# RetNet attention and a gated MLP on one core: the two heads of a pair change places in every second chunk

## The chip, the cores and the metric

The kernel runs on one core of a Trainium2 chip. The core has TensorE (PE; its weight loads are listed as PEld), VectorE (DVE), ScalarE (ACT), GpSimd (POOL) and a sync engine (SP) that issues most DMAs. The metric is the device time of one execution in microseconds; lower is better.

## The reference

Eight sequences of 576 positions with 8 heads of 64 go through a retention layer: scores with a decay per head, no softmax. The result, 512 wide, goes through a gated MLP whose gate mixes the positions of a sequence, with a residual.

```python
gamma = 1.0 - 2.0 ** (-5.0 - np.arange(H))
Dmat = np.where(rel >= 0, gamma[:, None, None] ** rel, 0.0)
x = concat_heads(np.matmul(scale * np.matmul(q, k.T) * Dmat, v))   # 8 x 576 x 512
h = gelu_tanh(x @ w_in)                                            # 512 -> 1024
u, v = h[..., :512], h[..., 512:]
v_n = (v - mean(v)) / sqrt(var(v) + 1e-6) * g_ln
v_s = einsum('ts,bsd->btd', w_sg, v_n) + b_sg[None, :, None]       # over positions
out = x + (u * v_s) @ w_out
```

## The kernel before, in words

**Blocks and chunks.** The positions are walked in 18 blocks of 256 rows. Blocks 0 and 9 are lead blocks: they hold the first 64 positions of four sequences each (32 partitions a sequence). Every other block holds 256 positions of one sequence, two blocks a sequence. A block's rows lie on 128 partitions, two neighbouring positions (a = 0, 1) on each. Partitions 0 to 63 are the block's chunk c = 0, partitions 64 to 127 its chunk c = 1, 128 positions each.

**Loads** (lines 76 to 91). Tile qk holds q and k of a block in float32, vf holds v. For a normal block each of q, k and v is one DMA of 512 KB into all 128 partitions, issued by SP (line 91); a lead block takes four DMAs of 128 KB, 32 partitions each (line 87; for block 0 the last two of q and of k go by ACT's queue). The pool has three buffers, and block j + 4 is loaded while block j is worked on: q first, k and v later in the step.

**Casts** (lines 257 to 274). GpSimd multiplies q and k by tables of decay powers, gq and gk, one value for each position and head, and writes bf16; v is copied to bf16. From block 3 on all of it is GpSimd's, in the order of the program, among small power operations for the norm (line 405, tile rs).

**Transposes.** q and k are needed with the head dimension on partitions. Two heads h = 2 kk + r, the pair kk, fill the 128 partitions: r = 0 on 0 to 63, r = 1 on 64 to 127. PE does it for the early blocks and for most of k (line 282, T); for q from block 5 and for k of the last three blocks it is a transposing DMA on SP (line 297, turn), which waits for the cast.

**Retention.** Four groups of products on PE use tiles of 64 by 64 of the 128 by 128 array. The row half of a tile is the half of the partitions that the operands are on, the column half is the half of the output's partitions.
- Sc (line 332): scores inside a chunk, rows r, columns c, so all four tiles. DVE multiplies them by the mask into ret (line 336).
- Z (line 357): adds k-transposed times v to a running state z in PSUM, a 64 by 64 matrix a head; head r on partitions 64 r to 64 r + 63. After each chunk the state is copied to bf16, tile zb (line 255, copy), by ACT for blocks below 5 and above 12 and by DVE between.
- inter (line 373): state times query, zb with qT into the output ot, chunk by chunk. Rows r and columns r for both chunks: two of the four tiles.
- intra (line 384): ret times v, added to ot; rows c, columns r.

ACT then copies ot to xT (line 390), the input of the MLP, with head r on its half of the partitions.

**MLP.** V (line 398) projects to the gate, U (line 460) to u, W (line 480) mixes positions, O (line 501) projects out and adds x (line 505, or on DVE at line 509).

**Order.** The order is written out by hand, and each engine works in that order. Lines 539 to 665 start the pipeline; the loop at lines 671 to 716 does for each block j: the transposing DMA of q of block j + 2, loads of block j + 4, intra(j), Sc and Z of the first chunk of j + 1, the cast of q of j + 3, then V, W and O pieces (run), U, inter(j + 1), Sc and Z of the second part, the casts of k and v. SP takes loads, transposing DMAs and stores in one queue.

Of the kernel before, what the change touches and what calls it, by code (L numbers as in the profile page):

```python
# [11 lines left out]
F32 = mybir.dt.float32  # L12
# [7 lines left out]
def kernel(  # L20
# [12 lines left out]
    nc = tc.nc  # L33
    B, H, S, D = q.shape
# [7 lines left out]
    NB = B // GB * NPG  # L42
# [5 lines left out]
    consts = ctx.enter_context(tc.tile_pool(name="consts", bufs=1))  # L48
# [13 lines left out]
    def place(j):  # L62

        gr, w = divmod(j, NPG)
        return (gr, None, 0) if w == 0 else (gr, GB * gr + (w - 1) // 2, (w - 1) % 2)

    def chunk(j, c):

        gr, b, half = place(j)
        if b is None:  # L70
            return 2 * gr + c, MID
        return b // 2, (MID + 1) * (b % 2) + 2 * half + c

    loaded = {}

    def load(j, parts=(k, q, v)):
        if j not in loaded:
            loaded[j] = ld.tile([128, 2, H, 2, D], F32, name="qk"), ld.tile([128, H, 2, D], F32, name="vf")
        qk, vf = loaded[j]
        gr, b, half = place(j)  # L80
        for dst, src in ((qk[:, 1], k), (qk[:, 0], q), (vf, v)):
            if src not in parts:
                continue
            if b is None:
                for x in range(GB):
                    eng = nc.scalar if j == 0 and x >= 2 and src is not v else nc.sync
                    eng.dma_start(dst[32 * x:32 * x + 32], src[GB * gr + x, :, :LEAD, :].rearrange(
                        "h (p a) d -> p h (a d)", a=2))
            else:
                s0 = LEAD + 256 * half  # L90
                nc.sync.dma_start(dst[:], src[b, :, s0:s0 + 256, :].rearrange("h (p a) d -> p h (a d)", a=2))  # L91

    load(0, (k, q))

# [32 lines left out]
    gq = consts.tile([128, 3, 2, H], F32, name="gq")  # L127
    gk = consts.tile([128, 3, 2, H], F32, name="gk")
    nc.scalar.activation(gk[:], prod[:], Act.Exp, scale=-1.0)
    nc.scalar.activation(gq[:], prod[:], Act.Exp, bias=lsc[:])  # L130
    load(0, (v,))
    w_stage = {}
    for half in (1, 0):
# [26 lines left out]
    wT = [consts.tile([128, S + LEAD], BF, name=f"wT{j}") for j in range(SB - 1)]  # L160
    wL = [consts.tile([128, S], BF, name=f"wL{e}") for e in range(2)]
    bp = consts.tile([SB * 2, 3, 64], BF, name="bp")

    def clear_wL():
        nc.gpsimd.memset(wL[0][64:], 0.0)
        nc.gpsimd.memset(wL[1][:64], 0.0)
        nc.gpsimd.memset(wnat[:, :, 0:64], 0.0)
# [31 lines left out]
    def build_wT(j):  # L199
        c0 = {"L0": 64, "L1": 0}.get(j) if isinstance(j, str) else 64 + LEAD + 128 * j  # L200
        tp = psS.tile([128, S], BF, name="wtp", tag="att")
        for t in range(SB):
            n = min(128, S - 128 * t)
            nc.tensor.transpose(tp[:, 128 * t:128 * t + n], wnat[:n, t, c0:c0 + 128], ident[:n, :n])
        if j == "L0":
            nc.vector.tensor_copy(wL[0][:64, :S - LEAD], tp[:64, LEAD:])
            nc.vector.tensor_copy(wL[0][:64, S - LEAD:], tp[:64, :LEAD])
        elif j == "L1":
            nc.vector.tensor_copy(wL[1][64:], tp[64:])
        else:  # L210
            e = nc.vector if j else nc.scalar
            copy(e, wT[j][:, :S], tp[:])
            copy(e, wT[j][:, S:], tp[:, :LEAD])
# [27 lines left out]
    xTs, uTs, gTs, vns, zbs = {}, {}, {}, {}, {}  # L241

    def xT(p, m):

        b = 2 * p + (m > MID)
        if m == MID:
            if (p, m) not in xTs:
                xTs[p, m] = xup.tile([128, KK, 128], BF, name="xm")
            return xTs[p, m]
        if b not in xTs:  # L250
            xTs[b] = xup.tile([128, MID, KK, 128], BF, name="xT")
        return xTs[b][:, m % (MID + 1)]

    def copy(eng, o, i):
        (eng.copy if eng is nc.scalar else eng.tensor_copy)(o, i)  # L255

    def cast(j, part, eng):
        s = blk.setdefault(j, {})
        qk, vf = loaded[j]
        b, half = place(j)[1:]  # L260
        kind = 0 if b is None else 1 + half
        if part == "q":
            dst, src, tab = w2.tile([128, 2, H, D], BF, name="qb"), qk[:, 0], gq
        else:
            pool = consts if b is None else w3
            dst = pool.tile([128, 2, H, D], BF, name=part + ("lead" if b is None else "b"))
            src, tab = (qk[:, 1], gk) if part == "k" else (vf[:], None)
        s[part + "b"] = dst
        o = dst[:].rearrange("p a h d -> p h a d")
        if tab is None:  # L270
            copy(eng, o, src)
        else:
            eng.tensor_tensor(o, src, tab[:, kind].rearrange("p a h -> p h a").unsqueeze(3).to_broadcast(  # L273
                [128, H, 2, D]), op=Alu.mult)
# [66 lines left out]
    def Z(j, c):  # L341

        gr, b, half = place(j)
        if b is None or (half, c) == (1, 1):
            nb = GB * gr if b is None else b + 1
            if c == 0 or nb == GB * (gr + 1):
                return
            src, lo, n, first = blk[NPG * gr], 32 * (nb % GB), 32, True
            zcur[0] = psZ.tile([128, KK, D], F32, name="zp")
        else:  # L350
            src, lo, n, first = blk[j], 64 * c, 64, False
        z, rows = zcur[0], slice(lo, lo + n)
        for a in range(2):
            for kk in range(KK):
                for r in range(2):
                    h = 2 * kk + r
                    nc.tensor.matmul(z[64 * r:64 * r + 64, kk, :], src["kb"][rows, a, h, :], src["vb"][rows, a, h, :],  # L357
                                     start=(first and a == 0 and kk == 0), stop=True, skip_group_check=True)
        zb = w3.tile([128, KK, D], BF, name="zb")
        copy(nc.scalar if j < 5 or j > NB - 6 else nc.vector, zb[:], z[:])  # L360
        zbs[(j, 1) if c == 0 else (j + 1, 0)] = zb

    def inter(j):
        s = blk[j]
        qT = s["qT"]
        s["ot"] = ot = [psO.tile([128, KK, 2, 64], F32, name="ot") for _ in range(2)]
        if place(j)[1] is None:
            return
        for kk in range(KK):
            for c in range(2):  # L370
                for r in range(2):
                    rr = slice(64 * r, 64 * r + 64)
                    nc.tensor.matmul(ot[c][rr, kk], zbs[j, c][rr, kk, :], qT[rr, :, kk, 64 * c:64 * c + 64],  # L373
                                     start=(kk == 0), stop=False, skip_group_check=True)

    def intra(j):
        s = blk[j]
        ret, vb, ot = s["ret"], s["vb"], s["ot"]
        ks = [(kk, a) for kk in (2, 3, 0, 1) for a in range(2)]
        for kk, a in ks:  # L380
            for c in range(2):
                for r in range(2):
                    cc = slice(64 * c, 64 * c + 64)
                    nc.tensor.matmul(ot[c][64 * r:64 * r + 64, kk], vb[cc, a, 2 * kk + r, :],  # L384
                                     ret[cc, r, kk, a, :],
                                     start=(place(j)[1] is None and (kk, a) == ks[0]),
                                     stop=True, skip_group_check=True)
        for c in range(2):
            x = xT(*chunk(j, c)).rearrange("p k (t a) -> p k a t", a=2)
            copy(nc.vector if j < 3 and c == 1 else nc.scalar, x, ot[c][:])  # L390
# [128 lines left out]
    def run(n):  # L519
        for _ in range(n):  # L520
            if wo:
                wo.pop(0)()

    def release(j):
        b, half = place(j)[1:]
        if b is None or half == 0:
            return
        ws = [lambda b=b, c=c, h=h: W(b, c, h) for h in range(2) for c in range(KK)]
        os = wo[2:]
        del wo[2:]  # L530
        while ws or os:
            wo.extend(ws[:2] + os[:1])
            ws, os = ws[2:], os[1:]
        p, e = divmod(b, 2)
        for m in ([MID] if e else []) + [(MID + 1) * e + x for x in range(MID)]:
            wo.append(lambda p=p, m=m: O(p, m))
# [18 lines left out]
    cast(1, "k", nc.gpsimd)  # L555
    spin(9)
    inter(0)
    intra(0)
    load(3)
    cast(1, "q", nc.vector)  # L560
# [19 lines left out]
    T(2, "k")  # L580
    spin(3)
    intra(1)
    T(2, "q")
    cen_of[0]()
# [50 lines left out]
    cast(3, "v", nc.gpsimd)  # L635
    build_wT(wb[4])
    build_wT(wb[5])
    release(2)
    run(1)
    T(3, "k")  # L640
# [112 lines left out]
```

## Time and profile before

| | |
|---|---|
| median of 3 runs | 222.45 us (220.46 to 222.47) |
| profiled execution: its time | 220.28 us |
| profiled execution: its span | 218.5 us |
| PE, DVE, POOL, ACT busy | 94%, 73%, 61%, 59% of the span |
| granted TensorE clock | 1.0 throughout |
| DMA moved | 47.47 MB, mean 217 GB/s |
| q and k loads of normal blocks | 16 each, 512 KB, median 6.2 and 7.0 us from issue to landing |

A row of a timeline or of a list of groups reads: start, duration, engine, line, operation, output<-inputs, shape, count. In a list of groups the parts behind the bars are busy time and mean ns of one, then the idle time of the engine before and what ended it. A row of the table of windows gives the stretch in us, its length, busy time of PE, PEld, DVE, ACT and POOL with counts, the granted clock, the DMA share and GB/s. The DMA share is the mean number of packets in flight over 16 engines, so it can be over 1.

### The profile page before, as it was taken

The numbers are of one execution on the slowest core, as the hardware profiler recorded it, in microseconds if no ns is written. First come the engines' busy times: TensorE is split into PE (matmuls) and PEld (weight loads), VectorE is DVE, ScalarE is ACT, GpSimd is POOL, SyncE is SP. The second block draws the span as 40 slices with busy tenths as digits, with TensorE's granted clock in tenths as the row PEclk, the third lists the DMA queues.
The fourth block names the chain that finished last, engine by engine and source line by source line (L and its number), as shares of the span: only waits on it lengthen the run. The fifth ranks groups of instructions, "written<-read, shape, count | busy, mean of one in ns | idle before, by whom it ended". The sixth has DMA issues, their size and how long they took to land.

```text
span 218.5 us, 8020 instructions
## 1 busy us (share of the span) xinstructions
PE 204.6 (94%) x3396; PEld 145.9 (67%) x3433; DVE 160.6 (73%) x347; ACT 128.3 (59%) x212; POOL 132.3 (61%) x136
## 2 busy tenths in 40 slices
PE   7897889898999999999999999999999999999990
PEld 2355567676777786777677776777867776676650
DVE  5467868785799798379857885858765887887771
ACT  5344468726577674947494948676667565465100
POOL 5187967899899598719582876758483911123000
PEclk9999999999999999999999999999999999999999
DMA  6999999999999899889979999989999982802335
GB/s 169 270 312 282 328 253 254 282 285 259 191 260 290 202 211 223 267 143 315 221 216 222 218 206 217 319 171 312 208 201 261 178 167 48 243 3 48 144 91 201
DMA packets 88180, 47.47 MB, mean 217 GB/s; under 512 B 26000, under 2 KB 82640, under 8 KB 88144
## 3 DMA queue, kind: packets, MB, share of 16 engines
q1 hardware_dynamic: 85440, 45.10, 90.2%
q0 software_dynamic: 1472, 1.20, 3.4%
q10 hardware_dynamic: 1232, 0.66, 1.2%
q8 instruction: 27, 0.44, 0.9%
q14 instruction: 9, 0.07, 0.1%
HBM read 32.79 MB, written 9.44 MB: 193 GB/s over the span
## 4 chain that ended last, share of the span: by engine, by line
PE 73%; DMA 6%; POOL 5%; issue 4%; DVE 4%; SPq 2%; ACT 2%; ACTq 1%; DVEq 0%; POOLq 0%
PE wp L480 17%; PE op L501 14%; PE hu L460 13%; PE hv L398 11%; DMA qk<-in_k_dram 4%; PE ot L384 4%; PE sc L332 4%; PE zp L357 4%; PE ot L373 3%; DMA qk<-in_q_dram 2%; PE op L505 2%; PE tp L282 2%; SPq L91 2%; POOL wnat L197 1%; POOL rs L405 1%
## 5 line engine op out<-in xcount | busy, mean ns | idle before, releaser
L405 POOL TENSOR_TENSOR rs<-rs,mhalf 128x1 f32<-128x1 f32 x36 | 31.6, 879 | 60.4 <-DVE rs L413 60.3
L336 DVE TENSOR_TENSOR ret<-sc,mask 128x512 bf16<-128x512 f32 x72 | 46.1, 682 | 11.9 <-PE sc L332 11.5
L480 PE MATMUL wp<-wT,vn 128*128 128x288 bf16 x256 | 41.7, 287 | 0.1
L482 DVE TENSOR_TENSOR gT<-wp,uT 128x288 bf16<-128x288 f32 x64 | 27.9, 450 | 12.8 <-PE wp L480 12.1
L460 PEld LDWEIGHTS <-w_in 128*128 128x128 bf16 x576 | 34.1, 98 | 3.2 <-issue 0.5
L501 PE MATMUL op<-w_out,gT 128*128 128x512 bf16 (+1 forms) x133 | 34.6, 373 | 1.1 <-issue 0.5
L409 DVE BATCH_NORM_STATS2 bst<-vg 128x6 f32<-128x512 f32 x36 | 24.8, 689 | 13.3 <-ACT vg L401 13.2
L460 PE MATMUL hu<-xT,w_in 128*128 128x128 bf16 x512 | 33.7, 219 | 0.2 <-DVE gT L482 0.2
L398 PE MATMUL hv<-w_in,xT 128*128 128x512 bf16 x111 | 31.5, 379 | 1.3 <-ACT xT L255 0.5
L273 POOL TENSOR_TENSOR kb<-qk,gk 128x1024 bf16<-128x1024 f32 x16 | 31.4, 1963 | 1.3 <-DMA qk<-in_k_dram 1.3
L401 ACT ACTIVATE vg<-hv 128x512 f32<-128x512 f32 x36 | 21.4, 595 | 15.4 <-PE hv L398 15.3
L422 DVE SCALAR_TENSOR_TENSOR vc<-vg,mv,g_bc 128x512 f32<-128x512 f32 x36 | 29.6, 823 | 0.0
L480 PEld LDWEIGHTS <-vn 128*128 128x128 bf16 x256 | 23.8, 98 | 8.0 <-ACT vn L434 0.7
L273 POOL TENSOR_TENSOR qb<-qk,gq 128x1024 bf16<-128x1024 f32 x15 | 28.9, 1928 | 0.0
L434 ACT ACTIVATE vn<-vc,rs 128x512 bf16<-128x512 f32 x32 | 23.1, 725 | 8.3 <-POOL rs L405 7.8
L463 ACT ACTIVATE uT<-hu 128x512 bf16<-128x512 f32 x32 | 19.2, 600 | 9.1 <-PE hu L460 8.9
L255 ACT CAST xT<-ot 128x512 bf16<-128x512 f32 x30 | 20.1, 740 | 6.4 <-PE ot L384 6.2
L501 PEld LDWEIGHTS <-gT 128*128 128x128 bf16 x148 | 12.9, 98 | 11.1 <-issue 0.3
L507 ACT COPY ob<-op 128x512 f32<-128x512 f32 x23 | 13.5, 588 | 10.6 <-PE op L505 10.4
L398 PEld LDWEIGHTS <-xT 128*128 128x128 bf16 x128 | 11.9, 98 | 9.9 <-DVE xT L255 0.5
L332 PE MATMUL sc<-qT,kT 64*64 64x128 bf16 x576 | 17.2, 219 | 1.4 <-DVE qT L255 0.7
L480 PE MATMUL wp<-wL,vnm 128*128 128x288 bf16 x64 | 18.4, 287 | 0.0
(104 smaller groups left out, 279.4 us busy)
## 6 DMA issues: line engine op xcount, KB each, us to landing
qk<-in_k_dram SPq DMA_DIRECT2D x16, 512.0 KB, 7.0
qk<-in_q_dram SPq DMA_DIRECT2D x16, 512.0 KB, 6.2
vf<-in_v_dram SPq DMA_DIRECT2D x16, 512.0 KB, 7.6
out_dram<-ob SPq DMA_DIRECT2D x20, 256.0 KB, 4.7
out_dram<-obs SPq DMA_DIRECT2D x11, 256.0 KB, 2.6
wst<-in_moe_w_in_dram SPq DMA_DIRECT2D x2, 1024.0 KB, 7.5
vf<-in_v_dram SPq DMA_DIRECT2D x8, 128.0 KB, 4.6
out_dram<-ob SPq DMA_DIRECT2D x8, 128.0 KB, 3.2
```

Of the source, the lines that this page charges most:

```text
L273: eng.tensor_tensor(o, src, tab[:, kind].rearrange("p a h -> p h a").unsqueeze(3).to_broadcast([128, H, 2, D]), op=Alu.mult)
L332: nc.tensor.matmul(sc[r][cc, x, a, :], kT[rr, a, kk, cc], qT[rr, :, kk, cc], start=True, stop=True, skip_group_check=True)
L336: nc.vector.tensor_tensor(s["ret"][:, r, 2 * g:2 * g + 2], sc[r][:], msk[:].unsqueeze(1).to_broadcast([128, 2, 2, 128]), op=Alu.mult)
L398: nc.tensor.matmul(hv[:], xT(p, m)[:, kk], w_in[:, kk, F2:], start=(kk == 0), stop=(kk == KK - 1))
L405: nc.gpsimd.tensor_tensor(st["rs"][:], st["rs"][:], mhalf[:], op=Alu.pow)
L409: nc.vector.bn_stats(bst[:], vg[:])
L422: nc.vector.scalar_tensor_tensor(vc[:], vg[:], mv[:, 0:1], g_bc[:], op0=Alu.subtract, op1=Alu.mult)
L434: nc.scalar.mul(vn[:], vc[:], rs[:])
L460: nc.tensor.matmul(hu[:, c, :], w_in[:, kk, 128 * c:128 * c + 128], xT(p, m)[:, kk], start=(kk == 0), stop=(kk == KK - 1), skip_group_chec ...
L480: nc.tensor.matmul(ps[:], vns[p, m][e][:, 128 * c:128 * c + 128], w, start=(x == 0), stop=(x == SB - 1))
L482: nc.vector.tensor_tensor(gTs[p][:, c, col:col + HS], ps[:], uTs[b][:, c, half * HS:half * HS + HS], op=Alu.mult)
L501: nc.tensor.matmul(op[:], gTs[p][:, c, r], w_out[:, c, f], start=(c == 0), stop=(xn is not None and c == KK - 1), skip_group_check=True)
```

## The change

For the normal blocks from block 4 on (TURNED), the two heads of each pair change places in the second chunk of q and k: on partitions 64 to 127 head 2 kk + 1 stands where 2 kk stood. The DMA does it: each q or k load becomes one DMA for partitions 0 to 63 and two for partitions 64 to 127, one for the even and one for the odd places. v stays. The tables of decay powers get a copy with the same exchange (turn_tables, six copies on GpSimd after the cast of v of block 3). Z takes k from the other place. The state that meets the second chunk is copied with its halves exchanged, in two copies of 64 partitions: one on the engine that copied it before, one on ACT. In inter the second chunk then has rows r and columns 1 - r, so its products use the other two tiles of the array. intra reads ret from the other place, and ot, xT and all behind it are as before.

```diff
+    TURNED = 4
+    def turned(j, c):
+        return c if j >= TURNED and place(j)[1] is not None else 0
...
-                nc.sync.dma_start(dst[:], src[b, :, s0:s0 + 256, :].rearrange("h (p a) d -> p h (a d)", a=2))
+                rows = src[b, :, s0:s0 + 256, :].rearrange("h (p a) d -> p h (a d)", a=2)
+                if j < TURNED or src is v:
+                    nc.sync.dma_start(dst[:], rows)
+                    continue
+                nc.sync.dma_start(dst[:64], rows[:64])
+                for r in range(2):
+                    nc.sync.dma_start(dst[64:, r::2], rows[64:, 1 - r::2])
...
+    def turn_tables():
+        for n, src in enumerate((gq, gk)):
+            gx[id(src)] = dst = consts.tile([128, 2, 2, H], F32, name=f"gx{n}")
+            nc.gpsimd.tensor_copy(dst[:64], src[:64, 1:])
+            for r in range(2):
+                nc.gpsimd.tensor_copy(dst[64:, :, :, r::2], src[64:, 1:, :, 1 - r::2])
...
+        if tab is not None and turned(j, 1):
+            tab, kind = gx[id(tab)], half
...
-                    nc.tensor.matmul(z[64 * r:64 * r + 64, kk, :], src["kb"][rows, a, h, :], src["vb"][rows, a, h, :],
+                    nc.tensor.matmul(z[64 * r:64 * r + 64, kk, :],
+                                     src["kb"][rows, a, h if first else 2 * kk + (r ^ turned(j, c)), :],
+                                     src["vb"][rows, a, h, :],
...
-        copy(nc.scalar if j < 5 or j > NB - 6 else nc.vector, zb[:], z[:])
+        eng = nc.scalar if j < 5 or j > NB - 6 else nc.vector
+        if c == 0 and turned(j, 1):
+            copy(eng, zb[:64], z[64:])
+            copy(nc.scalar, zb[64:], z[:64])
+        else:
+            copy(eng, zb[:], z[:])
...
-                    nc.tensor.matmul(ot[c][rr, kk], zbs[j, c][rr, kk, :], qT[rr, :, kk, 64 * c:64 * c + 64],
+                    e = 64 * (r ^ turned(j, c))
+                    nc.tensor.matmul(ot[c][e:e + 64, kk], zbs[j, c][rr, kk, :], qT[rr, :, kk, 64 * c:64 * c + 64],
...
-                                     ret[cc, r, kk, a, :],
+                                     ret[cc, r ^ turned(j, c), kk, a, :],
...
     build_wT(wb[5])
+    turn_tables()
```

More of the change, by code (lines that the diff above doesn't have):

```diff
@@ L130 @@
     nc.scalar.activation(gq[:], prod[:], Act.Exp, bias=lsc[:])
+    gx = {}
     load(0, (v,))
```

## The prediction, made before the changed kernel ran

> **What bounds the kernel now.** I read the page first (busy shares, slices, chain), then the PE timeline around one state-query product, then the table of windows for the DMA, then SP's timeline with the landings.
>
> ```profile
> span 218.5 us, 8020 instructions
> ...
> PE 204.6 (94%) x3396; PEld 145.9 (67%) x3433; DVE 160.6 (73%) x347; ACT 128.3 (59%) x212; POOL 132.3 (61%) x136
> ...
> PE   7897889898999999999999999999999999999990
> ...
> DMA  6999999999999899889979999989999982802335
> ...
> PE 73%; DMA 6%; POOL 5%; issue 4%; DVE 4%; SPq 2%; ACT 2%; ACTq 1%; DVEq 0%; POOLq 0%
> ```
>
> TensorE is busy in nine tenths or more of every slice from 55 us to 205 us and carries 73% of the chain, so a saving on PE there is a saving in time as long as nothing else is late. The second thing to see is the DMA row: eight or nine tenths in nearly every slice until about 175 us, although DMA has only 6% of the chain. It is nearly a second bound, hidden by loads that are issued a step early.
>
> The profiled execution took 220.28 us, 1.8 more than its span; it lies 2.2 below the median of 222.45 and close to the lowest run, 220.46. My sum starts from 220.28. A difference under about 1% (2.2 us) can't be told from no change here.
>
> **The saving.** One call of inter, with the scores and state products behind it, and a product elsewhere that fills all four 64x64 tiles of the array:
>
> ```profile
> 85.02 0.52 PE L373 MATMUL ot<-qT,zb 64*64 64x128 bf16 x12
> 85.33 0.24 PE L332 MATMUL sc<-qT,kT 64*64 64x128 bf16 x2
> ...
> 85.43 0.22 PE L373 MATMUL ot<-qT,zb 64*64 64x128 bf16 x2
> ...
> 86.06 1.04 PE L501 MATMUL op<-w_out,gT 128*128 128x512 bf16 x3
> ```
> ```profile
> 92.09 0.39 PE L332 MATMUL sc<-qT,kT 64*64 64x128 bf16 x16
> ```
>
> Today both chunks use the two diagonal tiles of the array, so 16 products start as 8 pairs: 85.02 to 85.43 in 7 steps, 0.058 us a pair. The four-at-once pattern that inter gets is the one that L332 has already: 16 products in 0.39, less 0.22 for the last one's own duration, 3 steps of 0.057. So a call shrinks from 8 steps to 4, by 0.23 us. What must be subtracted is overlap: the first L332 products start at 85.33, on the idle tiles, before inter ends. But the diagonal tiles still have their own L332 and L357 work afterwards, so L501 at 86.06 waits for them; shortening the diagonal's queue by 4 steps moves L501 by all of it. Blocks 4 to 17 without the lead block 9 are 13 calls: 13 x 0.23 = 3.0 us.
>
> [...]
>
> **Edits on other engines.**
>
> ```profile
> L255 ACT CAST zb<-zp 128x256 bf16<-128x256 f32 x18 | 6.8, 377 | 11.1 <-PE zp L357 11.1
> L454 POOL COPY uT<-um 128x256 bf16<-128x256 bf16 x8 | 3.1, 393 | 0.0
> L172 POOL CAST bp<-left 10x64 bf16<-10x64 f32 x2 | 0.5, 226 | 0.1
> ```
> ```profile
> 46.93 1.93 POOL L273 TENSOR_TENSOR qb<-qk,gq 128x1024 bf16<-128x1024 f32 x1
> ```
> ```profile
> 49.62 0.61 PE L282 MATMUL tp<-ident,qb 128*128 128x128 bf16 x8
> ```
>
> The 13 split copies of zb keep 256 elements per partition, so each half lasts as long as a whole: 13 x 0.377 = 4.9 us more on ACT; DVE, where it had a whole copy, has a half of the same length. ACT is 59% busy and mostly waits for PE; the state is read only after a projection and a gate product. I take 0; without that cover it is up to +4.9. The halves stand behind the xT copies, so ACT does not wait for Z where it didn't before; what queues behind is the next gate or ob, 0.4 later. The changed indices in Z, intra and the casts cost nothing: same shapes, same counts.
>
> The six table copies stand on POOL ahead of block 4's casts. From 226 ns at 64 elements and 393 at 256 I get about 198 at 32 and 184 at 16: 2 x 198 + 4 x 184 = 1.13 us (ends: 0 and 6 x 393 = 2.4). POOL finishes qb(4) at 48.86 and PE transposes it at 49.62: cover 0.76, so +0.37 us (ends 0 and 1.6).
>
> **The loads, which decide.** Each q and k load from block 4 on becomes three DMAs: partitions 0 to 63, then twice partitions 64 to 127 with half the heads. That is 52 more issues on SP. The rows that resemble them are the lead loads, 128 KB into 32 partitions:
>
> ```profile
> 77.50 1.93 SPq L87 DMA_DIRECT2D vf<-in_v_dram  x4
> ```
> ```profile
> 2.50:3.50 1.00, 1.00 (x4) 0.39 (x3) 0.93 (x4) 0.80 (x1) 1.00 (x3) 1.00 1.13 329
> 77.00:82.00 5.00, 5.00 (x110) 4.27 (x109) 4.86 (x11) 3.59 (x6) 4.79 (x7) 1.00 1.11 203
> 106.00:111.00 5.00, 4.95 (x78) 3.50 (x77) 4.02 (x10) 3.22 (x6) 3.74 (x3) 1.00 1.21 291
> 30.00:50.00 20.00, 18.72 (x324) 14.86 (x324) 16.39 (x39) 12.71 (x23) 16.02 (x17) 1.00 1.11 275
> 50.00:70.00 20.00, 19.11 (x407) 14.28 (x410) 16.17 (x34) 13.54 (x24) 18.77 (x15) 1.00 1.15 245
> 70.00:90.00 20.00, 19.75 (x347) 14.73 (x340) 16.21 (x35) 13.74 (x23) 15.35 (x16) 1.00 1.09 232
> 90.00:110.00 20.00, 19.79 (x332) 14.61 (x335) 15.02 (x32) 12.65 (x22) 12.56 (x10) 1.00 1.03 228
> 110.00:130.00 20.00, 19.57 (x369) 14.69 (x371) 15.30 (x35) 13.75 (x23) 13.01 (x12) 1.00 1.01 208
> 130.00:150.00 20.00, 19.58 (x372) 14.59 (x374) 13.71 (x30) 15.10 (x26) 12.76 (x12) 1.00 1.08 249
> 150.00:170.00 20.00, 19.84 (x374) 15.00 (x375) 13.46 (x31) 13.04 (x24) 12.21 (x10) 1.00 1.15 230
> ```
>
> The last two columns are the DMA share and GB/s. From 106 to 111 us only whole 128-partition loads run: 291 GB/s at a share of 1.21, the engines full. From 77 to 82 us the lead's k and v parts run one after another from SP: 203 GB/s, though the engines are hardly less occupied (1.11) and the issue (0.48 us for 128 KB, some 270 GB/s) is faster. From 2.5 to 3.5 us the same kind of parts come from two queues at once, SP filling the first 64 partitions and ACT the last 64: 329 GB/s. So neither size nor source makes them slow; a stream into one half of the partitions is slow. A split load fills one half, then the other: 524 KB at 203 is 2.58 us against 1.80 at 291, +0.78 (ends: 0, and no row gives more). 26 loads: +20.3 us of DMA time.
>
> [...]
>
> What can hide it: the seven windows from 30 to 170 us have a mean share of 1.09; against 1.21 that leaves 140 x (1 - 1.09/1.21) = 14 us spare. Spare can be used only where a load is already issued, so 14 is its upper end. By 166 us, 13.6 of it has passed and the queue is 20.3 - 13.6 = 6.7 us late. Who waits next:
>
> ```profile
> 166.38 3.54 SPq L297 DMA_TRANSPOSE kT<-kb  x1
> ...
> 174.77 1.29 SPq L297 DMA_TRANSPOSE kT<-kb  x1
> ```
> ```profile
> kT<-kb SPq DMA_TRANSPOSE x1, 5.5
> ```
> ```profile
> 174.24 0.39 PE L332 MATMUL sc<-qT,kT 64*64 64x128 bf16 x16
> ```
>
> kT of block 16 is issued behind the loads, lands at 166.38 + 5.5 = 171.9 and is read at 174.24: slack 2.4. So the scores of block 16 come 6.7 - 2.4 = 4.3 us late. Whatever inter has saved before that point is spent waiting; only the calls of blocks 16 and 17 come after it, 2 x 0.23 = 0.5. Sum: 4.3 - 0.5 = +3.8, 224.1 us. The table copies and part of the waiting fall earlier and are inside that number. The early sign of it is qT of block 5:
>
> ```profile
> 52.62 1.34 SPq L297 DMA_TRANSPOSE qT<-qb  x1
> ```
> ```profile
> DMA to landing us min/median/max: 6.3/6.3/6.3
> ```
> ```profile
> 60.27 0.39 PE L332 MATMUL sc<-qT,kT 64*64 64x128 bf16 x16
> ```
>
> Seven split loads stand ahead of it, 7 x 0.78 = 5.5 us, less 1.7 spare before 50 us (20 x (1 - 1.11/1.21)): 3.8 late against a slack of 60.27 - 58.9 = 1.4, so about 2.4 us of PE waiting there.
>
> **The rivals.** (1) Loads keep the whole-load rate; the saving arrives: -3.0 + 0.4 = -2.6, 217.7 us. For it: DMA has only 6% of the chain, so loads are rarely waited for. Against it: the 203 GB/s row. It needs an extra under about 0.2 us a load. (2) The slowness of the lead parts is a price per DMA, (0.65 - 0.45) = 0.2 us for each extra one (128 KB at 203 against 291): 52 x 0.2 = 10.4 in all. With half of the spare used, 6.8, the end is 3.6 - 2.4 = 1.2 late, less 0.5: +0.7, 221.0 us; with all of it used, (1)'s time. Against it: the engines stay occupied between the parts, share 1.11. (3) ACT becomes the late one: 13 x 0.377 = 4.9 in full, less 2.6: +2.3, 222.6. It decides from the point where the gate's PSUM tiles come free late; ACT's 41% idle speaks against it. (4) Four at once does not come about: inter's 0.23 stays, the DMA's lateness remains, 224.6.
>
> **How the numbers follow.** Forecast and (4), which end in the DMA, 0.5 and 0.03; (1) 0.2; (2) 0.2; (3) 0.07. The range takes (1) at its lower end, 217.6. At the upper end half of the spare can't be used: 4.3 + 6.8 - 0.5 = +10.6, 231. The forecast's own range is 221.5 to 231. Faster by over 1% is (1): 0.2. Within 1%: (2) and a little of the forecast's low end, 0.25. Slower: 0.55.
>
> **What would show it.** In the changed profile: L373 in a span of about 0.4 with four starts per 0.057 (saving right); ACT zb at 377 ns in halves; windows of q and k loads near 200 GB/s, and q and k landings later by a growing amount; waits of POOL casts for DMA of several us; PE waiting at L332 near 60 and 175 us. If split loads run at 290 GB/s, the forecast is wrong and (1) holds.

## The result and the profile after

The changed kernel took 237.09 us in the median of all its runs (233.31 to 239.16, 4 runs), the kernel before 221.57 beside it. The ratios here and below leave out executions in a disturbed, slower state, which here are two of the four runs, the profiled one (238.78 us) among them, so amounts below are taken from the experiments where they can be. The ratio of the other two (233.31 and 235.40) is 1.058 with an interval of 1.044 to 1.072. The forecast was 224.1, with 231 as its upper end.

The page of the changed kernel:

```profile
span 236.9 us, 8115 instructions
...
PE 207.3 (87%) x3396; PEld 145.4 (61%) x3433; DVE 161.2 (68%) x347; ACT 133.7 (56%) x225; POOL 132.4 (56%) x142
...
PE   8697798989459999999999979989999469999992
...
PEclk9999999999758999999999999999999959999999
DMA  6999999999999999999999999999999992452227
...
PE 40%; DMA 16%; DVE 14%; POOL 9%; ACT 9%; issue 5%; SPq 4%; ACTq 1%; DVEq 0%; POOLq 0%
```

PE's busy time is 2.7 us more than before while the span grew by 18.4: PE does hardly more work, it waits, and in two places, near 60 us and near 190 us (the 45 and the 46 in its row). In both the granted clock falls as well, to 0.50 from 63 to 72 us and from 189 to 195. The DMA row is full from the second slice to the thirty-third; before, it had eights and sevens in it.

PE's timeline, at these two places and at one ordinary call of inter:

```profile
67.52 0.64 PE L355 MATMUL sc<-qT,kT 64*64 64x128 bf16 x16 [3.46 <-ACT xT L276]
...
95.40 0.42 PE L404 MATMUL ot<-qT,zb 64*64 64x128 bf16 x16
95.65 0.39 PE L355 MATMUL sc<-qT,kT 64*64 64x128 bf16 x16
...
191.75 0.64 PE L355 MATMUL sc<-qT,kT 64*64 64x128 bf16 x16 [5.23 <-DMA kT<-kb]
```

Block 5's scores come at 67.52 (before 60.27), block 16's at 191.75 (before 174.24). Between them the call of inter does what the change says: 0.42 from the first start to the last end, less 0.22 for the last product's own duration, is 0.20 for 16 products, where before they took 0.42 from first start to last.

The list of waits (total, times, longest, us), and the table of windows:

```profile
DVE ret L359 <- PE sc L355: 23.8, 13, 7.6
...
ACT vn L465 <- POOL rs L436: 14.0, 10, 6.1
...
POOL qb L296 <- DMA qk<-in_q_dram: 7.1, 2, 5.4
ACT zb L276 <- DVE zb L276: 6.8, 6, 2.0
...
PE sc L355 <- DMA kT<-kb: 5.2, 1, 5.2
...
PE sc L355 <- ACT xT L276: 3.5, 1, 3.5
...
PE op L532 <- DMA w_out<-in_moe_w_out_dram: 2.9, 1, 2.9
```
```profile
43.00:53.00 10.00, 9.08 (x208) 7.14 (x206) 7.20 (x14) 4.13 (x7) 9.77 (x13) 1.00 1.20 191
50.00:70.00 20.00, 12.61 (x251) 9.35 (x255) 9.36 (x19) 8.45 (x15) 14.62 (x13) 0.82 1.24 186
67.00:69.50 2.50, 1.64 (x34) 1.39 (x36) 1.29 (x2) 1.01 (x2) 2.50 (x3) 0.50 1.21 191
```

The list names ACT's copy xT as what ended PE's wait of 3.5 us for block 5's scores. POOL and ACT around 60 us:

```profile
55.91 1.03 POOL L276 CAST vb<-vf 128x1024 bf16<-128x1024 f32 x1
62.29 1.93 POOL L296 TENSOR_TENSOR qb<-qk,gx 128x1024 bf16<-128x1024 f32 x1 [5.35 <-DMA qk<-in_q_dram]
...
64.52 0.56 POOL L436 TENSOR_TENSOR rs<-rs,mhalf 128x1 f32<-128x1 f32 x1
```
```profile
65.11 0.72 ACT L465 ACTIVATE vn<-vc,rs 128x512 bf16<-128x512 f32 x1 [6.12 <-POOL rs L436]
...
66.68 1.33 ACT L276 CAST xT<-ot 128x512 bf16<-128x512 f32 x2
```

POOL stands at q of block 6, which has not landed and which PE doesn't use until much later. Behind it in POOL's queue is a small power operation (rs) of another block; ACT's vn waits for that; and behind vn in ACT's queue is the copy xT. So one late load holds up two queues. But PE's scores don't need xT: in the kernel before they start at 60.27, while the products (L384, 59.80 to 60.44) that xT copies are still running. What they need is qT of block 5. Its transposing DMA is issued at 61.42 here (52.62 before) and takes 6.0 us to land, at 67.4, when the first of the two xT copies ends as well. So the wait is the one for qT, as in the run with the loads alone below, and the copies hide behind it: they are done at 68.0, and their reader, V, starts at 70.62. The wait for w_out just ahead (2.9) hides in it too: without it PE would have stood longer at the scores.

### The profile page after: what moved, and what is told of

It reads as the page before. It is cut to its first block, busy times and chain, and to the rows that moved or that the text cites. A ratio compares the mean times of both kernels' runs of the same rounds, so it can differ in the third digit from the quotient of the medians.

```text
span 236.9 us, 8115 instructions
## 1 busy us (share of the span) xinstructions
PE 207.3 (87%) x3396; PEld 145.4 (61%) x3433; DVE 161.2 (68%) x347; ACT 133.7 (56%) x225; POOL 132.4 (56%) x142
## 4 chain that ended last, share of the span: by engine, by line
PE 40%; DMA 16%; DVE 14%; POOL 9%; ACT 9%; issue 5%; SPq 4%; ACTq 1%; DVEq 0%; POOLq 0%
PE op L532 10%; PE wp L511 9%; PE hu L491 6%; DMA qk<-in_q_dram 6%; PE hv L429 6%; DMA qk<-in_k_dram 4%; DVE ret L359 4%; POOL kb L296 3%; DVE bst L440 3%; DMA kT<-kb 3%; DVE vc L453 3%; POOL rs L436 2%; SPq L100 2%; DVE gT L513 2%; DMA vf<-in_v_dram 2%
## 5 line engine op out<-in xcount | busy, mean ns | idle before, releaser
L436 POOL TENSOR_TENSOR rs<-rs,mhalf 128x1 f32<-128x1 f32 x36 | 30.9, 859 | 71.1 <-DVE rs L444 71.1
L511 PE MATMUL wp<-wT,vn 128*128 128x288 bf16 x256 | 42.8, 291 | 0.9 <-ACT ob L538 0.6
L532 PE MATMUL op<-w_out,gT 128*128 128x512 bf16 (+1 forms) x133 | 35.3, 379 | 4.7 <-DMA w_out<-in_moe_w_out_dram 2.9
L429 PE MATMUL hv<-w_in,xT 128*128 128x512 bf16 x111 | 32.6, 391 | 1.4 <-ACT xT L276 0.5
L296 POOL TENSOR_TENSOR qb<-qk,gx 128x1024 bf16<-128x1024 f32 x13 | 25.1, 1931 | 7.1 <-DMA qk<-in_q_dram 7.1
L453 DVE SCALAR_TENSOR_TENSOR vc<-vg,mv,g_bc 128x512 f32<-128x512 f32 x36 | 29.0, 808 | 0.0
L296 POOL TENSOR_TENSOR kb<-qk,gx 128x1024 bf16<-128x1024 f32 x13 | 25.1, 1931 | 0.1
L276 ACT CAST xT<-ot 128x512 bf16<-128x512 f32 x30 | 20.1, 737 | 7.3 <-PE ot L415 7.2
L355 PE MATMUL sc<-qT,kT 64*64 64x128 bf16 x576 | 15.4, 223 | 9.7 <-DMA kT<-kb 5.2
L276 ACT CAST zb<-zp 64x256 bf16<-64x256 f32 (+1 forms) x31 | 11.4, 368 | 22.0 <-PE zp L380 15.0
```

The costliest lines, as they stand in the source:

```text
L429: nc.tensor.matmul(hv[:], xT(p, m)[:, kk], w_in[:, kk, F2:], start=(kk == 0), stop=(kk == KK - 1))
L436: nc.gpsimd.tensor_tensor(st["rs"][:], st["rs"][:], mhalf[:], op=Alu.pow)
L453: nc.vector.scalar_tensor_tensor(vc[:], vg[:], mv[:, 0:1], g_bc[:], op0=Alu.subtract, op1=Alu.mult)
L511: nc.tensor.matmul(ps[:], vns[p, m][e][:, 128 * c:128 * c + 128], w, start=(x == 0), stop=(x == SB - 1))
L532: nc.tensor.matmul(op[:], gTs[p][:, c, r], w_out[:, c, f], start=(c == 0), stop=(xn is not None and c == KK - 1), skip_group_check=True)
```

## Experiments

Ratios are to the kernel before on the same chip, with a 95% interval; times are medians of all runs. Line numbers are each kernel's own, and `...` stands for lines left out.

**The loads alone.**

```diff
-                nc.sync.dma_start(dst[:], src[b, :, s0:s0 + 256, :].rearrange("h (p a) d -> p h (a d)", a=2))
+                rows = src[b, :, s0:s0 + 256, :].rearrange("h (p a) d -> p h (a d)", a=2)
+                if j < 4 or src is v:
...
+                nc.sync.dma_start(dst[:64], rows[:64])
+                for r in range(2):
+                    nc.sync.dma_start(dst[64:, r::2], rows[64:, r::2])
```


> The kernel before with q and k loads of normal blocks from block 4 on cut into the same three DMAs as in the change, heads in their old places; nothing else. Theory D and theory N (each further DMA costs, whatever partitions it fills): 232 to 240 us, as slow as the change or up to 3 us slower, with PE waiting near 60 us for the scores of block 5 and with q and k streaming at 185 to 205 GB/s. Theory S: 220 to 222 us.

Measured: 238.84 us, ratio 1.076 [1.068, 1.083], so the loads alone cost 16.7 us (0.0756 x 221). PE's timeline:

```profile
67.20 0.64 PE L338 MATMUL sc<-qT,kT 64*64 64x128 bf16 x16 [6.58 <-DMA qT<-qb]
...
188.88 0.64 PE L338 MATMUL sc<-qT,kT 64*64 64x128 bf16 x16 [6.08 <-DMA kT<-kb]
```

These are the two places that the prediction named, qT of block 5 and kT of block 16, with about 6.5 and 6 us of waiting. Set against the kernel before, a later product of block 5's step is 8.5 late (72.61 against 64.10), the same place in block 15's step 8.4 (177.61 against 169.23), the one in block 16's 16.8 (195.63 against 178.82). So nothing at all is lost in the 105 us between; each place costs 8.4.

Most of what the waits leave of the 8.4 is the granted clock behind them. At the first place PE comes to the scores 6.9 later than before (67.20 against 60.27) and to the product hv behind them 8.4 later (70.30 against 61.94); the granted clock is 0.50 from 67.2 to 70.2 us and 0.80 in the us after. At the second, 6.2 of the second loss is there at the scores (188.88 against 174.24, less 8.4) and all of it at the product hu (194.34 against 177.52); the clock is 0.50 from 188 to 193 us and 0.76 in the us after.

**The same three DMAs in number and size, but cut by heads, each over all 128 partitions; and cut into even and odd partitions.**

```diff
...
+                nc.sync.dma_start(dst[:, :4], rows[:, :4])
+                nc.sync.dma_start(dst[:, 4:6], rows[:, 4:6])
+                nc.sync.dma_start(dst[:, 6:], rows[:, 6:])
```


> The kernel before with the same loads cut into three DMAs of the same sizes (256, 128 and 128 KB), but by heads, so that each fills all 128 partitions. Theory D: 220 to 223 us, q and k at about 290 GB/s. Theory N: 230 to 240 us, as the cut by partitions.

```diff
...
+                nc.sync.dma_start(dst[0::2], rows[0::2])
+                for r in range(2):
+                    nc.sync.dma_start(dst[1::2, r::2], rows[1::2, r::2])
```


> The kernel before with the loads cut into three DMAs of the same sizes, but into every second partition: the even ones, then the odd ones in two parts. Theory D (what counts is the half of the array that is filled): 220 to 223 us, the rate of whole loads. If 64 partitions a DMA make it slow, wherever they lie: 232 to 240 us.

Measured: by heads 221.69 us, 0.999 [0.994, 1.004]; by every second partition 223.7 us, 1.006 [1.000, 1.011], where PE waits 2.05 us for w_out at 60.36. The window from 43 to 53 us, in which loads of blocks 4 to 6 make up most of the traffic (w_out's load begins at 50), of the kernel before, of the change's cut, of the cut by heads and of every second partition:

```profile
43.00:53.00 10.00, 9.08 (x206) 7.17 (x205) 7.74 (x15) 4.46 (x7) 9.98 (x8) 1.00 1.16 285
```
```profile
43.00:53.00 10.00, 9.44 (x210) 7.52 (x209) 7.75 (x15) 4.38 (x7) 8.27 (x7) 1.00 1.01 190
```
```profile
43.00:53.00 10.00, 9.44 (x209) 7.48 (x209) 7.82 (x15) 4.38 (x7) 9.98 (x8) 1.00 1.14 278
```
```profile
43.00:53.00 10.00, 9.49 (x211) 7.45 (x209) 7.89 (x15) 4.39 (x7) 9.98 (x8) 1.00 1.02 264
```

285, 190, 278 and 264 GB/s. The number of DMAs and their 64 partitions cost little; that the 64 are one half of the partitions is what costs. The rates are those of the whole stream, v loads included; why one half of the partitions is slower no run shows.

**The second half's DMAs from ACT's queue** (both copies of the state on one engine), to have both halves of the array filled at once.

```diff
-                    nc.sync.dma_start(dst[64:, r::2], rows[64:, 1 - r::2])
+                    nc.scalar.dma_start(dst[64:, r::2], rows[64:, 1 - r::2])
```


> The changed kernel complete, with the two loads of partitions 64 to 127 issued from ACT's queue beside SP's load of partitions 0 to 63, and both halves of a state copy on one engine. Theory D (a stream into one half of the partitions is slow; two streams into both halves at once are not): 218 to 224 us, q and k at about 290 GB/s or more while both streams run, less what 52 issues cost on ACT. If the slowness belonged to each DMA of 64 partitions whatever runs beside it: 230 us or more.

Measured: 245.44 us, 1.106 [1.099, 1.114], a miss: 189 GB/s from 40 to 50 us and 162 from 60 to 70. ACT's DMA issues stand in its own queue (two took 2.08 us at 41.93) and came 1.5 and 3 us after SP's for the same loads (q at 41.93 against 40.38, k at 39.54 against 36.43), so the halves did not start at once. Whether two halves together keep the rate is left open.

**Everything but the loads.** The change with whole loads, so that the exchange in memory is left out; then the same with both copies of the state on the engine that had the whole one.

```diff
-                if j < TURNED or src is v:
+                if True:
```


> The changed kernel with whole q and k loads of 512 KB again: the exchange of the heads is left out of the loads, so q and k of second chunks are taken in the old places while the tables, the state, inter and intra exchange them; its output is another one. Theory D (loads into one half of the partitions at a time are slow, and the DMA becomes the bound): 217 to 219 us against some 221 before, with all of the 13 x 0.22 us of inter saved less at most 1 us for the tables and the split state copies. Theory S (the split copies on ACT, the tables or the four tiles cost the time): stays at 230 us or more.

```diff
-            copy(nc.scalar, zb[64:], z[:64])
+            copy(eng, zb[64:], z[:64])
```


> The changed kernel with whole loads (the exchange left out of the loads, so its output is another one) and with both halves of a state copy on the engine that made the whole copy before. Theory A (in blocks 5 to 12 ACT's half waits for DVE's half, and with it everything behind it on ACT): 217 to 219.5 us, the 2.9 us of inter arriving. Theory P (the six table copies push GpSimd's casts into the way of DVE, and that is what cost the whole-load kernel 6 us): stays at 224 us or more.

Measured: 228.2 us, 1.032 [1.025, 1.040]; and 227.22, 1.012 [1.001, 1.022], where the ratio rests on two runs (225.76 and 223.10). Neither is at or below the kernel before, as had been expected if the loads were all. So something besides the loads costs 3%, about 7 us, and the second copy on ACT looks like a good part of it. The waits of the first:

```profile
ACT zb L276 <- DVE zb L276: 9.3, 6, 4.5
...
PE ot L404 <- DVE zb L276: 2.2, 1, 2.2
```

ACT's half waits for DVE's half, six times, with the whole of ACT's queue behind it. The longest of the six, 4.5, and PE's 2.2 both end near 67.4 us and have another cause as well: a DVE operation, vc, that lasts 5.62 there (60.09 to 65.71). The tables are behind that, as the next but one experiment shows.

**The split copy alone, in the kernel before.**

```diff
...
+        if c == 0 and j >= 4 and b is not None:
+            copy(eng, zb[:64], z[:64])
+            copy(nc.scalar, zb[64:], z[64:])
...
```


> The kernel before with only the split of the state copies, nothing exchanged: one half on the engine as before, one on ACT. Theory A: 225 to 231 us, with ACT's copies of zb waiting for DVE's for several us in all. Theory P: 220 to 223 us.

Measured: 224.9 us, 1.012 [1.005, 1.019]: +2.7 us for copies that the prediction had at 0. Again ACT waits for DVE's half (5.2 us, 6 times).

**The table copies: moved to POOL's idle time at the start; and alone in the kernel before.**

```diff
+    turn_tables()
+
     def clear_wL():
...
     build_wT(wb[5])
-    turn_tables()
```


> The change with whole 512 KB loads (so the exchange of heads in memory is left out and other numbers are computed), both halves of zb on the engine that made the whole copy, and the six small table copies moved to the start of POOL's program, where POOL stands idle from 3.8 to 10.3 us. With the tables late this kernel had a ratio of 1.012. Theory P (the tables' 1.2 us push POOL's casts of block 4 and after onto DVE's centring at 60 us, a vc of 5.6 us): the casts of block 4 start at about 45.0 again, no vc of over 3 us near 60 us, and the saving of 13 x 0.22 = 2.8 us shows: ratio 0.985 to 0.998. Rival R (the 0.2 us that each second half of zb costs DVE, or the changed pattern itself, is what costs): ratio stays 1.005 to 1.02.

> The kernel before, with the six table copies on POOL at the place where the change has them; nothing reads them. Theory P: POOL's casts of block 4 start 1.2 us later, a vc of over 4 us stands near 60 us, and the ratio is 1.006 to 1.02. Rival R: the tables are hidden, or cost their 0.37 us: ratio 0.998 to 1.004.

Measured: the change without the loads' part, with both copies of the state on one engine and with early tables 223.41 us, 1.0085 [1.005, 1.012], not the 0.985 to 0.998 expected if the tables were the rest; the tables alone 224.59, 1.012 [1.007, 1.018], so 2.7 us for 1.2 us of POOL's time. DVE's timeline near 60 us, before and with the tables alone, and a wait of PE's in the second:

```profile
59.85 1.88 DVE L422 SCALAR_TENSOR_TENSOR vc<-vg,mv,g_bc 128x512 f32<-128x512 f32 x1
```
```profile
61.76 5.63 DVE L430 SCALAR_TENSOR_TENSOR vc<-vg,mv,g_bc 128x512 f32<-128x512 f32 x1
```
```profile
PE ot L381 <- DVE zb L263: 2.3, 1, 2.3
```

The same operation that took 0.74 us at 58.12 in the kernel before lasts 5.63, and PE waits 2.3 us for the state that DVE copies behind it. The run with whole loads, late tables and both copies on one engine has it too (DVE, then POOL):

```profile
60.08 5.63 DVE L453 SCALAR_TENSOR_TENSOR vc<-vg,mv,g_bc 128x512 f32<-128x512 f32 x1
```
```profile
59.84 1.93 POOL L296 TENSOR_TENSOR kb<-qk,gx 128x1024 bf16<-128x1024 f32 x1
...
63.24 1.93 POOL L296 TENSOR_TENSOR qb<-qk,gx 128x1024 bf16<-128x1024 f32 x1
69.17 0.92 POOL L436 TENSOR_TENSOR rs<-rs,mhalf 128x1 f32<-128x1 f32 x1 [4.00 <-DVE rs L444]
```

vc ends at 65.71, 0.54 after the last of POOL's operations that follow one another from 59.84 to 65.17. In the kernel before POOL has no gap either:

```profile
59.26 1.92 POOL L273 TENSOR_TENSOR kb<-qk,gk 128x1024 bf16<-128x1024 f32 x1
61.13 1.50 POOL L255 CAST vb<-vf 128x1024 bf16<-128x1024 f32 x1
```

There vc ends at 61.73, and it is POOL's vb that lasts longer, 1.50 instead of the usual 1.03. Which of the two engines gives way, and why, no run here shows. With the tables at the start vc is 1.88 again (at 59.79). That POOL's casts are what holds DVE up is inferred from their lying side by side. And PE, with the tables alone:

```profile
61.23 1.04 PE L509 MATMUL op<-w_out,gT 128*128 128x512 bf16 x4 [0.85 <-DMA w_out<-in_moe_w_out_dram]
```

The load of w_out is issued by POOL behind the casts of block 4. In the kernel before it is issued at 49.78, takes 8.0 us to land, and is first read at 58.62: under 1 us of slack. Issued later by the tables it is what PE waits for (2.9 us in the complete change); in the run with early tables it took 9.7 us to land, and PE waited 1.6.

**w_out out of the way; then both copies of the state on ACT; and a control.**

```diff
     pow_of[4]()
+    load_w(SB)
...
     cast(4, "v", nc.gpsimd)
-    load_w(SB)
```


> The run with whole loads (exchange in memory left out), tables at the start and both halves of zb on one engine, and now the load of w_out issued from POOL at about 38 us instead of behind the casts of block 4. In the run without this, PE waited 1.56 us at 58.5 us for w_out, which in the kernel before lands just ahead of its first reader. Theory W (that wait is most of its loss): no wait of PE for w_out, ratio 1.0085 less 0.007, so 0.997 to 1.004. Rival V (the wait only moves, because DVE or the DMA are late next): the w_out wait is gone but the ratio stays 1.006 to 1.012.

> As the run with w_out early, but both halves of the exchanged zb on ACT in blocks 5 to 12, so DVE loses 8 copies of 0.41 us and ACT takes 16 of 0.38. Theory DVE (at 73 to 74% DVE is what PE, arriving 0.22 us earlier a block, waits for: gT and zb): PE's waits for DVE gT go, ratio 0.985 to 0.996. Rival ACT (ACT's longer queue delays the gate and xT): ratio 1.002 to 1.012, waits of PE for ACT. Rival none (neither): within 0.003 of the run with w_out early.

> The kernel before with the load of w_out issued at about 38 us, nothing else: the control for the two others. The kernel before does not wait for w_out, so both theories expect 0.997 to 1.003; the 0.85 us that POOL spends at 38 us are in a stretch where it is idle.

Measured: 221.39 us, 1.002 [0.998, 1.005]; 221.29, 0.998 [0.996, 1.001]; control 221.04, 0.998 [0.995, 1.001]. With loads, tables and w_out put aside the change is level with before, whichever engine has the copies. DVE and PE in the run with both copies on DVE:

```profile
83.29 0.86 DVE L278 CAST zb<-zp 64x256 bf16<-64x256 f32 x2
84.18 0.82 DVE L515 TENSOR_TENSOR gT<-wp,uT 128x288 bf16<-128x288 f32 x2
```
```profile
84.69 1.02 PE L534 MATMUL op<-w_out,gT 128*128 128x512 bf16 x4 [0.54 <-DVE gT L515]
```

and in the control:

```profile
83.21 0.41 DVE L255 CAST zb<-zp 128x256 bf16<-128x256 f32 x1
83.55 0.81 DVE L482 TENSOR_TENSOR gT<-wp,uT 128x288 bf16<-128x288 f32 x2
```

The second copy moves gT back by 0.6, and PE's next product waits 0.54 for it: more than the 0.217 that the call of inter saves. Over the whole run PE waits 1.9 us for gT, in the control 0.2. With both copies on ACT it waits 0.2 for gT again; what takes the saving there isn't shown.

**PE's saving alone.** inter writes the second chunk to the other half, and nothing else is changed, so the exchange of the heads that belongs to it is left out; then the same with the early w_out.

```diff
+                    e = 64 * (r ^ (c if j >= 4 and place(j)[1] is not None else 0))
-                    nc.tensor.matmul(ot[c][rr, kk], zbs[j, c][rr, kk, :], ...
+                    nc.tensor.matmul(ot[c][e:e + 64, kk], zbs[j, c][rr, kk, :], ...
```


> The kernel before with one part of the change alone: inter writes the second chunk's output to the other half of the partitions in blocks 4 to 17, so it runs four at once. No exchange in the loads, the tables, the state or the output is made, so heads are added up in the wrong place (that part of the computation is left out): nothing but PE's saving is left. Theory Z (the saving is real, and what the state's second copies cost on DVE or ACT eats it): 13 x 0.217 = 2.8 us less what PE then waits for, ratio 0.986 to 0.993. Rival K (PE is held back by DVE, ACT and loads anyway, so a saving on PE alone is worth little): 0.995 to 1.002.

> The same with the load of w_out issued from POOL at about 38 us. Theory Z: at or up to 0.003 below the run without it, 0.985 to 0.992. Rival K: 0.994 to 1.001.

Measured: 218.89 us, 0.990 [0.987, 0.994]; 219.68, 0.993 [0.990, 0.996]. PE's timeline of the first:

```profile
84.86 0.42 PE L374 MATMUL ot<-qT,zb 64*64 64x128 bf16 x16
85.11 0.39 PE L332 MATMUL sc<-qT,kT 64*64 64x128 bf16 x16
...
85.69 1.04 PE L502 MATMUL op<-w_out,gT 128*128 128x512 bf16 x3
```

L502 comes 0.83 after inter's start; before, L501 came 1.04 after it (85.02, 86.06). The saving is time: 2.1 us of the 13 x 0.217 = 2.8. Of the rest PE stands 0.65 before the scores of block 16, for kT (at 173.61).

**Another way to four at once.** inter and intra put the second chunk's output into exchanged halves, and the copy xT puts it right in two copies of 64 partitions; loads, tables and state stay.

```diff
...
+            if c and place(j)[1] is not None:
+                copy(eng, x[:64], ot[c][64:])
+                copy(eng, x[64:], ot[c][:64])
...
```


> Another way to four products at once, on the kernel before: loads, casts, scores and states stay, inter and intra write the second chunk's two heads to exchanged halves of ot in all 16 normal blocks, and the copy from ot to xT exchanges them back in two copies of 64 partitions for that chunk (16 x 0.74 us more on ACT or DVE). Theory D: 217 to 220 us, faster than before by 16 x 0.22 less what ACT's longer copies delay. Theory S (ACT's copies count): 222 to 228 us.

Measured: 224.7 us, 1.015 [1.009, 1.021]. ACT spends 32.3 us on xT copies (44) instead of 20.1 (30). That these copies are the loss here too is likely, but no run takes them away alone.

**The complete change with the tables at the start and both copies of the state on one engine; and the same from block 10 on only.**

```diff
-    TURNED = 4
+    TURNED = 10
```


> The complete change with its split loads, but the tables at the start and both halves of zb on one engine: the two side costs are taken away and the loads are left. Theory D (the loads are the bound, so what the other engines save or lose is spent waiting): ratio 1.05 to 1.075, 233 to 238 us, not distinguishable from the change or a little below it. Rival S (the parts add up): the change's 1.058 less about 0.03 for the side costs, so 1.02 to 1.035, 226 to 229 us.

> As the run with the loads left, but heads change over from block 10 on: 16 split loads instead of 26, all of them issued after about 80 us, 8 calls of inter with four at once. At 1.0 us of DMA time more for each split load that is 16 us. If the spare of 1 - 1.09/1.21 of the time, some 9 us over 90 us, can be used, and 2.4 us of slack, the end is 5 us late less 0.4: ratio about 1.02. If the spare can't be used because loads are issued only when buffers come free: 16 - 2.4 = 13 us, ratio about 1.06. If it is the early collision at 50 to 70 us that costs the change its time: ratio 0.99 to 1.005.

Measured: 237.96 us, 1.078 [1.071, 1.086]; 230.67, 1.034 [1.025, 1.044]. Taking away the tables' and ACT's cost gains nothing while the loads are split, so the parts don't add up: in the changed kernel the waits for w_out (2.9) and for block 5's scores (3.5) come one behind the other, 6.4 in all, and with the loads alone the second by itself is 6.6. That this run and the loads alone (1.076) lie above the change's own 1.058 shows no order among the three: the change's ratio rests on two runs, and its four runs (233.31 to 239.16) overlap with the loads' (236.51 to 239.48). From block 10 on, 16 split loads, the early place is not touched and the late one is:

```profile
PE sc L357 <- DMA kT<-kb: 5.1, 1, 5.1
```

No version ran faster than the kernel before, apart from those that leave out part of the computation.

## Why the prediction was right and wrong

- **The saving** was right in kind and size: 0.217 us a call, forecast 0.23, and 0.990 when it is alone. Four at once does come about (0.20 for 16 products instead of 0.42), so rival (4) falls.
- **"So neither size nor source makes them slow; a stream into one half of the partitions is slow."** Right, and the other cuts show it; rivals (1) and (2) fall. So is the place: qT of block 5 and kT of block 16.
- **"A split load fills one half, then the other: 524 KB at 203 is 2.58 us against 1.80 at 291, +0.78."** This is the step that failed: the term was mis-sized. It took v at the whole-load rate, but the whole stream, v included, runs at 190 GB/s: three loads of a block take 3 x 524 / 190 = 8.3 us against 5.5 at 285, so +1.4 for each split load and not 0.78. What part of that falls on v and what on the split loads, no run separates. In the prediction's own sum 26 x 1.4 = 36, less 13.6 spare and 2.4 slack, is 20 us late; the loads alone cost 16.7. Read back from the landings the term is 1.2 to 1.4. With the loads alone qT of block 5 is issued 8.2 us later than before (60.79 against 52.62): with the 1.7 of spare 9.9 for 7 loads. kT of block 16 lands 17.0 later (188.9 against 171.9): with the 13.6 of spare 30.6 for 26 loads. From block 10 on it lands 10.0 later (181.9): with 8.5 of spare from 80 us on 18.5 for 16 loads. The 203 came from five us of the lead loads, the only such row, and was taken as the upper end of the cost because "no row gives more"; the top of the range, 231, moved only the spare, not the rate.
- **The early sign** came, 6.6 us of waiting with the loads alone where 2.4 was forecast, by the same rate. In the complete change PE waits 3.5 there, behind 2.9 for w_out. POOL also stops, at q of block 6, with rs, vn and xT behind it, which the prediction did not follow; PE's wait hides it.
- **A wait was taken at its own length.** The prediction put nothing for the half clock behind it; with the loads alone 6.6 and 6.1 us of waiting cost 8.4 each.
- **"I take 0 ... ACT does not wait for Z where it didn't before."** Wrong: ACT waits for DVE's half, and the copy alone costs 2.7 us. With both copies on DVE the second (0.42 us) delays gT by more than the 0.217 saved; with both on ACT (0.37) the time comes out level as well. Rival (3), that the copies decide, was given 0.07; it priced them at 4.9 in full.
- **The tables**: 1.13 us forecast, 1.2 us measured on POOL, but +2.7 where 0.37 (up to 1.6) was forecast. The step looked only at the next reader, qb(4), and not at what stands behind in POOL's queue: the load of w_out, with under 1 us of slack, and casts that now lie over DVE's vc, behind which PE waits 2.3.
- Not settled: why vc lasts 5.63 us beside POOL's casts in some runs and 1.88 in others, and what takes the saving when ACT has both copies of the state.

## What to carry to other kernels

Here a stream of loads of which two in three were cut into halves of the partitions ran at two thirds of the rate (190 against 285 GB/s) with the same bytes; cut by heads it kept 278. So cut a load by another dimension first. A copy that restores a layout cost DVE as much for 64 partitions as for 128 (420 and 414 ns). It has to be weighed against the saving on PE as if it stood on PE's path: in this kernel, with PE at 94%, the other engines hand over just in time. For an operation put into a full queue, list all that stands behind it with its slack, DMA issues first, not only its own reader.

## What was not expected of the hardware

- After a wait of PE of some 6 us the granted clock is 0.50 for the next three to five (the window from 67.0 to 69.5 us above, and the two places of the run with the loads alone), and 16 score products last 0.64 us instead of 0.39. At the first place of that run the clock is back within the us from 70.2, some 3 us after the scores start (67.20); at the second within the us from 193, nearer 5 (188.88). In the changed kernel it is 0.50 already before the second wait ends, from 189 us with the scores at 191.75, and 1.00 from 196. What sets the length of these stretches no run shows.
- A DVE operation of 0.74 us lasted 5.63 while POOL's casts ran one after another, across three casts and a small operation; in the kernel before it lasted 1.88 and one of POOL's casts 1.50 instead of 1.03.
